# Masked attention scores turned by the DMA crossbar instead of TensorE, with longer leads and loads in smaller steps

## The chip, the cores and the metric

One core of one Trainium2 chip. The metric is the device time of one execution in microseconds (us), the median of several runs.

The profile names the engines PE (TensorE), DVE (VectorE), ACT (ScalarE), POOL (GpSimd) and SP (SyncE). SP only issues DMAs here, one after the other in the order of the program. The DMA share is the time that packets took, as a share of 16 DMA engines; the granted clock is the share of its full clock that TensorE was given.

## The reference, cut to what matters

```python
batch, n_heads, seq, head_dim = 8, 8, 576, 64          # attention
n_tokens, d_model, d_ff = 4608, 512, 2048              # dense layers

scores = scale * np.matmul(q, k.transpose(0, 1, 3, 2))
thresh = np.max(scores, axis=-1, keepdims=True) - tau   # tau = 0.02
scores = np.where(scores >= thresh, scores, -1e9)
attn = np.exp(scores - max)                             # then divided by its sum
x = np.matmul(attn, v)                                  # heads side by side: 4608 x 512
h = x @ w_in
out = (h - np.tanh(h)) @ w_out
```

## The kernel before

It works through 32 pairs of heads. A pair has nine tiles of 128 query rows by 576 keys: four "duos" (an A and a B tile) and one middle tile M made of the remaining rows of both heads. For each tile TensorE computes scores, VectorE scales them and takes the row maximum, and ScalarE masks with a very steep Prelu (`kink`): a score above the threshold passes, one below becomes hugely negative. The masked scores `z` must then be turned, so that keys lie on partitions, before the product with v. Before the change TensorE turns them through an identity matrix into PSUM, and ScalarE takes the exponential from there:

```python
AHEAD = 3                       # scores run three tiles ahead
ps_z = pool("ps_z", 1, space=PSUM)
ps_h = pool("ps_h", 1, space=PSUM)
# ...
def weights(i):
    kd = kind(i % TPP)
    ps = ps_z.tile([P, 5 * P], BF16, name="psZ", tag="z")
    # ... z, pt, off, n by kind of tile: n is 4 (A, M) or 5 (B) ...
    for c in range(n):
        nc.tensor.matmul(
            out=ps[:, c * P : (c + 1) * P],
            lhsT=z[:, off + c * P : off + (c + 1) * P],
            rhs=ident_bf, is_transpose=True, start=True, stop=True,
        )
    # ... one more, half as high, for M ...
    nc.scalar.activation(
        out=pt[:, off : off + n * P], in_=ps[:, 0 : n * P], func=ACT.Exp
    )
# ... per tile s:
scores(s + AHEAD); kink(s + 1); weights(s)
# ... one step of the dense layers: 4 matmuls, then tanh and shrink at once ...
attend(s - 1)                   # product with v
```

From the fifth pair on (tile 39), one step of the dense layers (four 512-column matmuls) is slipped in after each tile; what is left of them follows as a tail. The weights are loaded in 16 pieces of 512 KB during the first 64 tiles. q, k and v come per pair, 256 KB each and the 64 remaining rows of each head apart; a copy of k with its halves swapped (`kS`) is made by two DMAs inside SBUF.

## Time and profile before

| | before |
|---|---|
| time, median of 3 runs | 647.22 us (646.89 to 647.35) |
| span of the profiled run | 644.8 us |
| busy PE / DVE / ACT | 594.6 / 459.5 / 461.6 us |
| attention alone ends (first dense matmul) | 78.1 us |
| tail of dense layers begins | 561.8 us |

The page's lines and the stage table are in the prediction. This is the group view of the hidden layer's matmuls in the kernel before; after the three durations (shortest, median, longest) stand the first and the last start:

```profile
L358 PE MATMUL psH<-xT,w_in_sb x451: 376/379/390, 78.1 to 615.0; 128*128 128x512 bf16 x151
L358 PE MATMUL psHt<-xT,w_in_sb x79: 379/379/379, 561.8 to 613.3; 128*128 128x512 bf16 x79
```

The first `psH` marks the end of the attention-only stage (78.1 us), and the first `psHt`, a buffer name used in the tail alone, the end of the main loop (561.8 us). So the dense stage lasts 483.7 us and the tail 83 us. This is the DMA queue's line of the page; its last figure is the time that its packets took as a share of the span of 16 engines:

```profile
q1 hardware_dynamic: 56662, 56.05, 30.8%
```

### The profile page before, as it was taken

Reading aid. Unit: us, or ns where it says so; the run is one execution under the profiler, and the core shown is the slowest. Engines: PE = TensorE matmul, PEld = TensorE weight load, DVE = VectorE, ACT = ScalarE, POOL = GpSimd, SP = SyncE. Lnnn points to the kernel's source line nnn. Section 1 sums busy time; section 2 is a strip of 40 time slices with the busy share of each in tenths; the row PEclk is TensorE's granted clock in tenths of the full one; section 3 lists DMA queues with packets and bytes.
Section 4 is the critical chain, followed back from the end, with each engine's and each line's share of the span. In section 5 each row is a group of like instructions: output and inputs, shape, how many; then the busy total and the mean of one; then the engine's idle time right before and its main releaser. Section 6 shows DMA issues by size and latency. Waiting matters only on the chain.

```text
span 644.8 us, 15693 instructions
## 1 busy us (share of the span) xinstructions
PE 594.6 (92%) x6048; PEld 362.0 (56%) x6130; DVE 459.5 (71%) x1274; ACT 461.6 (72%) x761; POOL 215.2 (33%) x309
## 2 busy tenths in 40 slices
PE   2988998989999999999999999999999999999990
PEld 2666655556566566656655656656665666544440
DVE  2888888887877777877778777877877777544410
ACT  1888888887778777787778787777778778533410
POOL 6267557733303730343313630362133400000000
PEclk9999999999999999999999999999999999999996
DMA  5565656432223331353133231353134201000111
GB/s 152 155 177 163 175 168 174 119 81 73 64 65 91 104 93 37 93 148 92 40 87 84 77 90 38 93 149 95 36 93 121 66 17 37 18 33 34 49 36 47
DMA packets 57139, 57.35 MB, mean 89 GB/s; under 512 B 20840, under 2 KB 45416, under 8 KB 57064
## 3 DMA queue, kind: packets, MB, share of 16 engines
q1 hardware_dynamic: 56662, 56.05, 30.8%
q8 instruction: 48, 0.79, 0.5%
q10 hardware_dynamic: 402, 0.29, 0.1%
q14 instruction: 27, 0.22, 0.1%
HBM read 37.75 MB, written 9.44 MB: 73 GB/s over the span
## 4 chain that ended last, share of the span: by engine, by line
PE 79%; ACT 9%; DVE 4%; issue 3%; DMA 2%; SPq 1%; ACTq 0%
PE psY L372 18%; PE psH L358 16%; PE psS L228 16%; PE psZ L269 10%; PE psO L313 5%; ACT pT L279 5%; ACT z L253 3%; PE ps_k L172 3%; PE psHt L358 3%; PE ps_q L172 2%; PE psS L218 2%; DVE sc L234 2%; PE psX L337 2%; DMA out_dram<-yo 2%; PE psO L301 1%
## 5 line engine op out<-in xcount | busy, mean ns | idle before, releaser
L279 ACT ACTIVATE pT<-psZ 128x512 f16<-128x512 bf16 (+1 forms) x288 | 184.6, 641 | 83.8 <-PE psZ L269 80.9
L253 ACT ACTIVATE z<-sc,nb 128x576 bf16<-128x576 f32 x288 | 221.3, 768 | 8.9 <-DVE nb L239 8.9
L234 DVE TENSOR_SCALAR_CACHE_REDUCE sc<-psS 128x576 f32<-128x576 f32 x288 | 216.2, 751 | 8.8 <-PE psS L228 7.8
L365 DVE SCALAR_TENSOR_TENSOR g<-th,psH 128x512 bf16<-128x512 f32 x124 | 85.3, 688 | 88.9 <-ACT th L364 88.9
L372 PE MATMUL psY<-w_out_sb,g 128*128 128x512 bf16 x540 | 138.2, 379 | 1.3
L269 PE MATMUL psZ<-ident_bf,z 128*128 128x128 bf16 x1280 | 118.8, 219 | 9.9 <-ACT pT L279 9.1
L358 PE MATMUL psH<-xT,w_in_sb 128*128 128x512 bf16 x451 | 118.1, 379 | 3.4 <-issue 1.3
L269 PEld LDWEIGHTS <-z 128*128 128x128 bf16 x1280 | 79.2, 98 | 52.2 <-issue 16.7
L228 PE MATMUL psS<-kT,qT 128*128 128x512 f16 (+1 forms) x512 | 105.8, 288 | 2.8 <-DVE qT L178 0.9
L228 PEld LDWEIGHTS <-qT 128*128 128x128 f16 x1024 | 74.2, 98 | 58.8 <-issue 5.2
L228 PE MATMUL psS<-kS,qT 128*128 128x512 f16 (+1 forms) x512 | 105.6, 288 | 0.0
L364 ACT ACTIVATE th<-psH 128x512 f32<-128x512 f32 x124 | 74.0, 597 | 35.9 <-PE psH L358 34.3
L146 POOL TENSOR_SCALAR xs<-kraw 128x576 f32<-128x576 f32 x31 | 20.8, 670 | 225.0 <-DMA kraw<-in_k_dram 159.1
L372 PEld LDWEIGHTS <-g 128*128 128x128 bf16 x576 | 51.8, 98 | 46.1
L358 PEld LDWEIGHTS <-w_in_sb 128*128 128x128 bf16 x576 | 51.0, 98 | 43.0 <-issue 0.8
L313 PEld LDWEIGHTS <-pT 128*128 128x128 f16 x1280 | 55.8, 98 | 22.4
L313 PE MATMUL psO<-vb,pT 128*128 128x65 bf16 x1280 | 61.2, 193 | 0.9
L239 DVE TENSOR_SCALAR nb<-mx 128x1 f32<-128x1 f32 x288 | 44.3, 154 | 10.0
L150 POOL TENSOR_TENSOR khl<-xs,khl 128x576 f16<-128x576 f32 x31 | 39.7, 1279 | 2.6
L150 POOL TENSOR_TENSOR qhl<-xs,qhl 128x576 f16<-128x576 f32 x31 | 39.6, 1279 | 2.6
L328 DVE TENSOR_TENSOR osb<-psO,rc 128x320 bf16<-128x320 f32 x64 | 29.3, 458 | 2.2
L178 DVE COPY qT<-ps_q 128x1152 f16<-128x1152 f16 x32 | 24.1, 754 | 9.2 <-PE ps_q L172 9.2
(53 smaller groups left out, 462.3 us busy)
## 6 DMA issues: line engine op xcount, KB each, us to landing
out_dram<-yo SPq DMA_DIRECT2D x36, 256.0 KB
kS<-kT SPq DMA_DIRECT2D x62, 144.0 KB
kraw<-in_k_dram SPq DMA_DIRECT2D x32, 256.0 KB
vraw<-in_v_dram SPq DMA_DIRECT2D x32, 256.0 KB
qraw<-in_q_dram SPq DMA_DIRECT2D x31, 256.0 KB
wt<-in_moe_w_in_dram SPq DMA_DIRECT2D x8, 512.0 KB
wt<-in_moe_w_out_dram SPq DMA_DIRECT2D x8, 512.0 KB
vraw<-in_v_dram SPq DMA_DIRECT2D x64, 32.0 KB
```

The source lines that it names most:

```text
L150: nc.gpsimd.tensor_tensor(out=hl[:, :, 1, :], in0=x, in1=hl[:, :, 0, :], op=ALU.subtract)
L228: nc.tensor.matmul(out=ps[:, dst], lhsT=lhs, rhs=kk[:, src], start=(n == 0), stop=(n == 1),)
L234: nc.vector.tensor_scalar(out=sc, in0=ps[:, lo : lo + S], scalar1=SC, scalar2=None, op0=ALU.mult, op1=ALU.max, accum_out=mx,)
L239: nc.vector.tensor_scalar(out=nb, in0=mx, scalar1=-1.0, scalar2=tau, op0=ALU.mult, op1=ALU.add)
L253: nc.scalar.activation(out=z, in_=sc, func=ACT.Prelu, bias=nb, scale=1.0, alpha=STEEP)
L269: nc.tensor.matmul(out=ps[:, c * P : (c + 1) * P], lhsT=z[:, off + c * P : off + (c + 1) * P], rhs=ident_bf, is_transpose=True, start=True ...
L279: nc.scalar.activation(out=pt[:, off : off + n * P], in_=ps[:, 0 : n * P], func=ACT.Exp)
L313: nc.tensor.matmul(out=po[:, (j - 1 - 5 * hh) + ab, :], lhsT=pt[:, blk * P : (blk + 1) * P], rhs=vb[:, hh, c, :], start=(n == 0), stop=(n ...
L358: nc.tensor.matmul(out=ps, lhsT=w_in_sb[:, c, n * P : (n + 1) * P], rhs=xT[:, c, m, 0:MB] if m < B else xT[:, c, :, MB:S], start=(c == 0), ...
L364: nc.scalar.activation(out=th, in_=ps, func=ACT.Tanh)
L365: nc.vector.scalar_tensor_tensor(out=gs[m][:, n, :], in0=th, scalar=-1.0, in1=ps, op0=ALU.mult, op1=ALU.add,)
L372: nc.tensor.matmul(out=ps, lhsT=gs[m][:, n, ms * P : (ms + 1) * P], rhs=w_out_sb[:, n, :], start=(n == 0), stop=(n == DF_C - 1),)
```

## The change

The intent is to free TensorE, the bound, from the 1312 turns: the DMA crossbar turns a duo of tiles at once, 128x1152, in SBUF, and one exponential reads the turned duo. A turn by DMA comes later than one by TensorE, so the masks now run five tiles ahead of the exponentials and the scores seven. Loads are spread, one tensor a tile; tanh and shrink are put off by a tile; the freed PSUM bank goes to the hidden layer. All loads (but the first q) and all stores stay on the SP queue, with the turns.

```diff
-    AHEAD = 3
+    AHEAD = 7
+    LDK = 16
+    MASK = 5
+    LAG = 2
-    ps_z = pool("ps_z", 1, space=PSUM)
-    ps_h = pool("ps_h", 1, space=PSUM)
+    ps_h = pool("ps_h", 2, space=PSUM)
@@ kink @@
         nc.scalar.activation(
             out=z, in_=sc, func=ACT.Prelu, bias=nb, scale=1.0, alpha=STEEP
         )
+        if kd != "A":
+            n = 5 if kd == "M" else TPP
+            t = zt_pool.tile([P, TPP, P], BF16, name="zT")
+            nc.sync.dma_start_transpose(
+                out=t[:, 0:n, :],
+                in_=zt,
+            )
+            zts[i] = t
@@ weights @@
-        for c in range(n):
-            nc.tensor.matmul(... is_transpose=True ...)      # cut
-        nc.scalar.activation(
-            out=pt[:, off : off + n * P], in_=ps[:, 0 : n * P], func=ACT.Exp
-        )
+        if kd != "A":
+            n = 5 if kd == "M" else TPP
+            pt = p_pool.tile([P, TPP * P], FP16, name="pT")
+            nc.scalar.activation(
+                out=pt[:, 0 : n * P], in_=zts.pop(i)[:, 0:n, :], func=ACT.Exp
+            )
+            pts[i] = pt
@@ main loop, per tile s @@
-        if 0 <= s + 1 < NTILE:
-            kink(s + 1)
+        if 0 <= s + MASK < NTILE:
+            kink(s + MASK)
+        bend()                       # tanh of the step before
         ...
+        shrink()                     # h - tanh(h) of the step before
-        if 0 <= s - 1 < NTILE:
-            attend(s - 1)
+        if 0 <= s - LAG < NTILE:
+            attend(s - LAG)
-            if j == 0 and p + 2 < NPAIR:
-                load(p + 2)          # k, q and v at once
+        for step in plan.pop(s, []): # one tensor's load, split or turn
+            step()
... (cut: nb of the threshold one tile later, x of the dense layers in two tiles,
     stores held back a step, more buffers, other PSUM buffers in the tail)
```

More of the change, by code (lines that the diff above doesn't have):

```diff
@@ L64 @@
     make_identity(nc, ident_bf)
-    xT = const.tile([P, DM_C, B, S], BF16, name="xT")
+    xR = const.tile([P, DM_C, B, S - 512], BF16, name="xR")
     w_in_sb = const.tile([P, DM_C, d_ff], BF16, name="w_in_sb")
     w_out_sb = const.tile([P, DF_C, d_model], BF16, name="w_out_sb")
-    NV = 3
+    NV = 4
     vbs = []
@@ L80 @@
         vbs.append(vb)
+    NM = 2
+    zms = []
+    for i in range(NM):
+        zm = const.tile([P, 5 * P], BF16, name=f"zm{i}")
+        nc.vector.memset(zm[:, S : 5 * P], -STEEP)
+        zms.append(zm)
     pool = lambda name, bufs, **kw: ctx.enter_context(
@@ L88 @@
     qk_pool = pool("qk", 2)
-    sc_pool = pool("sc", AHEAD + 1)
-    st_pool = pool("st", 8)
-    z_pool = pool("z", 3)
+    sc_pool = pool("sc", AHEAD - MASK + 2)
+    st_pool = pool("st", 12)
+    z_pool = pool("z", 4)
+    zt_pool = pool("zt", 4)
     p_pool = pool("p", 3)
@@ L97 @@
     y_pool = pool("y", 2)
+    x_pool = pool("x", 2)
     ps_big = pool("ps_big", 2, space=PSUM)
-    ps_z = pool("ps_z", 1, space=PSUM)
     ps_o = pool("ps_o", 1, space=PSUM)
-    ps_h = pool("ps_h", 1, space=PSUM)
+    ps_h = pool("ps_h", 2, space=PSUM)
     ps_y = pool("ps_y", 1, space=PSUM)
@@ L107, with load @@
     raws = {}
-    def load(p):
+    def load(p, t):
         b, h0 = p // HPAIR, 2 * (p % HPAIR)
         hs = slice(h0, h0 + 2)
-        for t, src in (("k", k), ("q", q)):
-            eng = nc.scalar if p == 0 and t == "q" else nc.sync
-            r = raw_pool.tile([P, 10, D], F32, name=f"{t}raw", tag=t)
-            eng.dma_start(
-                out=r.rearrange("p (h c) d -> p h (c d)", h=2)[:, :, 0 : 4 * D],
-                in_=src[b, hs, 0:512, :].rearrange("h (p c) d -> p h (c d)", c=4),
-            )
-            eng.dma_start(out=r[:, 4, :], in_=src[b, hs, 512:S, :])
-            raws[p, t] = r
-        r = raw_pool.tile([P, 10, D], F32, name="vraw", tag="v")
-        nc.sync.dma_start(
-            out=r[:, 0:8, :].rearrange("p (h c) d -> p h (c d)", h=2),
-            in_=v[b, hs, 0:512, :].rearrange("h (p c) d -> p h (c d)", c=4),
-        )
-        rem = v[b, hs, 512:S, :].rearrange("h s d -> s h d")
-        nc.sync.dma_start(out=r[0:64, 8:10, :], in_=rem)
-        nc.sync.dma_start(out=r[64:P, 8:10, :], in_=rem)
-        raws[p, "v"] = r
+        src = {"k": k, "q": q, "v": v}[t]
+        eng = nc.scalar if p == 0 and t == "q" else nc.sync
+        r = raws[p, t] = raw_pool.tile([P, 10, D], F32, name=f"{t}raw", tag=t)
+        n = 8 if t == "v" else 10
+        eng.dma_start(
+            out=r[:, 0:n, :].rearrange("p (h c) d -> p h (c d)", h=2)[:, :, 0 : 4 * D],
+            in_=src[b, hs, 0:512, :].rearrange("h (p c) d -> p h (c d)", c=4),
+        )
+        if t == "v":
+            rem = src[b, hs, 512:S, :].rearrange("h s d -> s h d")
+            eng.dma_start(out=r[0:64, 8:10, :], in_=rem)
+            eng.dma_start(out=r[64:P, 8:10, :], in_=rem)
+        else:
+            eng.dma_start(out=r[:, 4, :], in_=src[b, hs, 512:S, :])
     hls = {}
@@ L200 @@
     REM = (slice(512, 576), slice(576, 640))
-    scs, zs, pts, ops = {}, {}, {}, {}
+    scs, zs, zts, pts, ops = {}, {}, {}, {}, {}
     def kind(j):
@@ L237, in scores, with shift @@
         )
+        scs[i] = sc, mx
+    def shift(i):
+        sc, mx = scs[i]
         nb = st_pool.tile([P, 1], F32, name="nb", tag="nb")
@@ L247, in kink @@
         if kd == "B":
-            z = zs[i - 1][:, S:W]
-        else:
-            zt = z_pool.tile([P, W], BF16, name="z")
-            zs[i] = zt
+            zt = zs.pop(i - 1)
+            z = zt[:, S:W]
+        elif kd == "A":
+            zt = zs[i] = z_pool.tile([P, W], BF16, name="z")
+            z = zt[:, 0:S]
+        else:
+            zt = zms[i // TPP % NM]
             z = zt[:, 0:S]
@@ L255, in kink @@
         )
+        if kd != "A":
[6 more added lines that the diff above has]
+            zts[i] = t
     def weights(i):
         kd = kind(i % TPP)
-        ps = ps_z.tile([P, 5 * P], BF16, name="psZ", tag="z")
-        if kd == "B":
-            z, pt, off, n = zs.pop(i - 1), pts[i - 1], 512, 5
-        else:
-            z = zs[i] if kd == "A" else zs.pop(i)
+        if kd != "A":
+            n = 5 if kd == "M" else TPP
             pt = p_pool.tile([P, TPP * P], FP16, name="pT")
+            nc.scalar.activation(
+                out=pt[:, 0 : n * P], in_=zts.pop(i)[:, 0:n, :], func=ACT.Exp
+            )
             pts[i] = pt
-            off, n = 0, 4
-        for c in range(n):
-            nc.tensor.matmul(
-                out=ps[:, c * P : (c + 1) * P],
-                lhsT=z[:, off + c * P : off + (c + 1) * P],
-                rhs=ident_bf, is_transpose=True, start=True, stop=True,
-            )
-        if kd == "M":
-            nc.tensor.matmul(
-                out=ps[0:64, 512:640], lhsT=z[:, 512:576],
-                rhs=ident_bf, is_transpose=True, start=True, stop=True,
-            )
-        nc.scalar.activation(
-            out=pt[:, off : off + n * P], in_=ps[:, 0 : n * P], func=ACT.Exp
-        )
-        if kd == "M":
-            nc.scalar.activation(
-                out=pt[0:64, 512:640], in_=ps[0:64, 512:640], func=ACT.Exp
-            )
     def attend(i):
@@ L306, in attend @@
             return
-        pt, hh = pts.pop(i - 1), int(j > 4)
+        pt, hh = pts.pop(i), int(j > 4)
         for ab in range(2):
@@ L331, in norm @@
         )
+    xs = {}
     def emit_x(p):
         o = osb.pop(p)
-        ps = ps_z.tile([P, S], BF16, name="psX", tag="z")
+        ps = ps_h.tile([P, S], BF16, name="psX", tag="h")
         for t in range(4):
@@ L348, in emit_x @@
         b = p // HPAIR
-        nc.vector.tensor_copy(out=xT[:, p % HPAIR, b, :], in_=ps)
-    gs = {}
+        if p % HPAIR == 0:
+            xs[b] = x_pool.tile([P, DM_C, MB], BF16, name="xT")
+        nc.vector.tensor_copy(out=xs[b][:, p % HPAIR, :], in_=ps[:, 0:512])
+        nc.vector.tensor_copy(out=xR[:, p % HPAIR, b, :], in_=ps[:, 512:S])
+    gs, stores = {}, []
     def hidden(m, n, ps):
@@ L359, in hidden, with bend, shrink @@
                 out=ps, lhsT=w_in_sb[:, c, n * P : (n + 1) * P],
-                rhs=xT[:, c, m, 0:MB] if m < B else xT[:, c, :, MB:S],
+                rhs=xs[m][:, c, :] if m < B else xR[:, c, :, :],
                 start=(c == 0), stop=(c == DM_C - 1),
             )
-        th = t_pool.tile([P, MB], F32, name="th")
-        nc.scalar.activation(out=th, in_=ps, func=ACT.Tanh)
-        nc.vector.scalar_tensor_tensor(
-            out=gs[m][:, n, :], in0=th, scalar=-1.0, in1=ps,
-            op0=ALU.mult, op1=ALU.add,
-        )
+        halves.append((m, n, ps))
+    halves, ths = [], []
+    def bend():
+        while halves:
+            m, n, ps = halves.pop(0)
+            th = t_pool.tile([P, MB], F32, name="th")
+            nc.scalar.activation(out=th, in_=ps, func=ACT.Tanh)
+            ths.append((m, n, ps, th))
+    def shrink():
+        while ths:
+            m, n, ps, th = ths.pop(0)
+            nc.vector.scalar_tensor_tensor(
+                out=gs[m][:, n, :], in0=th, scalar=-1.0, in1=ps,
+                op0=ALU.mult, op1=ALU.add,
+            )
     def project(m, ms, part, ps, last):
@@ L383, in project @@
                 rows = out[m * S : m * S + MB, :].rearrange("(p c) n -> c p n", c=4)
-                nc.sync.dma_start(out=rows[ms], in_=yo)
+                to = rows[ms]
             else:
                 rows = out.rearrange("(b s) n -> b s n", b=B)
-                nc.sync.dma_start(out=rows[2 * ms : 2 * ms + 2, MB:S, :], in_=yo)
+                to = rows[2 * ms : 2 * ms + 2, MB:S, :]
+            stores.append(lambda: nc.sync.dma_start(out=to, in_=yo))
     def layers(m, tail):
@@ L393, in h_step @@
         def h_step(n):
-            if tail and n % 3:
+            if tail and n % 2:
                 ps = ps_big.tile([P, MB], F32, name="psHt", tag="big")
@@ L401, in y_step @@
             if part == 0:
-                tag = ("y", "o", "z")[(4 * (m - 1) + ms) % 3] if tail else "y"
-                pl = {"y": ps_y, "o": ps_o, "z": ps_z}[tag]
+                tag = ("y", "o")[ms % 2] if tail else "y"
+                pl = {"y": ps_y, "o": ps_o}[tag]
                 cur["y"] = pl.tile([P, d_model], F32, name="psY", tag=tag)
@@ L440, in w_load @@
         loaded.append((flat, wt, i, cols))
-    load(0)
-    load(1)
+    PREP = (
+        (LDK, lambda p: load(p, "k")),
+        (LDK - 1, lambda p: load(p, "q")),
+        (LDK - 2, lambda p: load(p, "v")),
+        (8, lambda p: split(p, "k")),
+        (7, lambda p: split(p, "q")),
+        (5, lambda p: turn(p, "k")),
+        (3, lambda p: turn(p, "q")),
+        (4, split_v),
+    )
+    plan = {}
+    for p in range(1, NPAIR):
+        first = TPP * p - AHEAD
+        for d, f in PREP[3 if p == 1 else 0 :]:
+            plan.setdefault(first - d, []).append(lambda p=p, f=f: f(p))
+    for t in ("k", "q", "v"):
+        load(0, t)
     for t in ("k", "q"):
@@ L448 @@
     split_v(0)
+    for t in ("k", "q", "v"):
+        load(1, t)
     pieces = w_pieces()
@@ L452 @@
     todo, stage = [], 0
-    for s in range(-AHEAD, NTILE + 4):
+    for at in sorted(plan):
+        if at < -AHEAD:
+            plan.setdefault(-AHEAD, []).extend(plan.pop(at))
+    for s in range(-AHEAD, NTILE + LAG + 3):
         p, j = divmod(max(s, 0), TPP)
-        if 0 <= s < NTILE and j == 3 and p % HPAIR == 0 and p >= HPAIR:
+        if 0 <= s < NTILE and j == 2 + LAG and p % HPAIR == 0 and p >= HPAIR:
             assert not todo
             todo = layers(stage, False)
-            share = len(todo) / (HPAIR * TPP - 3)
+            share = len(todo) / (HPAIR * TPP - 2 - LAG)
             done, stage = 0.0, stage + 1
-        if s + AHEAD < NTILE:
+        if 0 <= s + AHEAD - 1 < NTILE:
+            shift(s + AHEAD - 1)
+        if 0 <= s + AHEAD < NTILE:
             scores(s + AHEAD)
-        if 0 <= s + 1 < NTILE:
-            kink(s + 1)
+        if 0 <= s + MASK < NTILE:
+            kink(s + MASK)
+        bend()
         if 0 <= s < NTILE:
@@ L473 @@
                     done -= 1
-        if s - 1 == NTILE + 1:
-            emit_x(NPAIR - 1)
-        if 0 <= s - 1 < NTILE:
-            attend(s - 1)
-            pp, jj = divmod(s - 1, TPP)
+        shrink()
+        for store in stores[:-1]:
+            store()
+        del stores[:-1]
+        if 0 <= s - LAG < NTILE:
+            attend(s - LAG)
+            pp, jj = divmod(s - LAG, TPP)
             if jj == 4:
@@ L482 @@
                 norm(pp, 1)
-            if jj == 1 and pp > 0:
-                emit_x(pp - 1)
-        if 0 <= s < NTILE:
-            if j == 0 and p + 2 < NPAIR:
-                load(p + 2)
-            if p + 1 < NPAIR:
-                if j == 0:
-                    split(p + 1, "k")
-                if j == 1:
-                    split(p + 1, "q")
-                if j == 2:
-                    split_v(p + 1)
-                    turn(p + 1, "k")
-                if j == 4:
-                    turn(p + 1, "q")
-            if s in w_when:
+        pp, jj = divmod(s - LAG, TPP)
+        if jj == 1 and 0 < pp <= NPAIR:
+            emit_x(pp - 1)
+        for step in plan.pop(s, []):
+            step()
+        if True:
+            if s + AHEAD in w_when:
                 if loaded:
@@ L507 @@
             step()
+            bend()
+            shrink()
+            for store in stores:
+                store()
+            stores.clear()
         stage += 1
```

## The prediction

> **What bounds the kernel now.** I read four views in this order: the page's busy times and slices, the table by stage, the costliest groups, and the chain that ended last in one steady stretch. The page first:
>
> ```profile
> PE 594.6 (92%) x6048; PEld 362.0 (56%) x6130; DVE 459.5 (71%) x1274; ACT 461.6 (72%) x761; POOL 215.2 (33%) x309
> PE   2988998989999999999999999999999999999990
> DVE  2888888887877777877778777877877777544410
> ACT  1888888887778777787778787777778778533410
> DMA  5565656432223331353133231353134201000111
> ```
>
> TensorE is busy 92% of the span; VectorE and ScalarE are next at 71 and 72%; the DMA engines are half busy for the first 120 us and a quarter to a third busy later. The page marks a busy PE as modelled, so I checked it by stage and against the chain.
>
> ```profile
> 20.00:60.00 40.00, 35.27 (x482) 24.78 (x480) 34.03 (x107) 36.24 (x61) 24.84 (x33) 1.00 0.62 179
> 200.00:300.00 100.00, 97.16 (x1041) 60.52 (x1054) 78.81 (x223) 78.94 (x130) 38.09 (x56) 1.00 0.32 86
> 500.00:560.00 60.00, 58.16 (x599) 35.29 (x607) 44.39 (x124) 46.33 (x77) 7.35 (x12) 1.00 0.11 32
> 560.00:600.00 40.00, 39.24 (x181) 17.87 (x185) 17.39 (x26) 14.43 (x25) 0.00 (x0) 1.00 0.11 39
> ```
>
> The columns are window and length, then busy time of PE, weight loads, DVE, ACT and POOL, then granted clock, DMA share and GB/s. Three stages show. Up to about 72 us there are four pairs of heads with attention alone, and ACT (36.2 of 40), PE and DVE are nearly level. From 72 to 558 us attention runs beside the two dense layers and PE alone is full (97 of 100, the two others at 79). From 560 us there are only dense layers, which the change hardly touches.
>
> ```profile
> L269 PE MATMUL psZ<-ident_bf,z 128*128 128x128 bf16 x1280 | 118.8, 219 | 9.9 <-ACT pT L279 9.1
> L253 ACT ACTIVATE z<-sc,nb 128x576 bf16<-128x576 f32 x288 | 221.3, 768 | 8.9 <-DVE nb L239 8.9
> L279 ACT ACTIVATE pT<-psZ 128x512 f16<-128x512 bf16 x160 | 94.8, 592 | 26.1 <-PE psZ L269 23.8 <-PE psZ L275 2.3
> L279 ACT ACTIVATE pT<-psZ 128x640 f16<-128x640 bf16 x128 | 89.8, 702 | 57.7 <-PE psZ L269 57.2
> L349 DVE COPY xT<-psX 128x576 bf16<-128x576 bf16 x32 | 14.5, 454 | 8.0 <-PE psX L344 8.0
> L365 DVE SCALAR_TENSOR_TENSOR g<-th,psH 128x512 bf16<-128x512 f32 x124 | 85.3, 688 | 88.9 <-ACT th L364 88.9
> ```
>
> These are the groups that the change touches: 1280 turns of masked scores on PE, the exponentials that read them from PSUM, and the copy and the shrink that are rearranged. The 118.8 us are not what PE would win, since each turn's 219 ns overlaps its neighbours. The chain in time order has the marginal cost:
>
> ```profile
> 303.04 0.49 PE psS L228 x4
> 303.53 0.22 PE psZ L269 x4
> 303.75 0.86 PE psH L358 x4
> ...
> 308.64 0.49 PE psS L228 x4
> 309.13 0.28 PE psZ L269 x5
> 309.41 0.86 PE psY L372 x4
> ```
>
> Four turns cost 0.22 us and five 0.28 us, so 55 ns each, and the chain stays on PE throughout.
>
> **What the Trainium skill says.** "TensorE: Matmul & The Clock Gate", section "Wait — 56ns, not 53.3ns?", gives 55.6 ns start to start for warm 128-column matmuls; the 0.22 us for four agrees. "DMA: Bandwidth & Descriptors", section "Latency and other measured facts", gives 261 GB/s as the effective rate of a DMA transpose, and the section "Anatomy of one DMA" about 2 us of fixed cost per DMA, measured there on the GpSimd path; no transpose is in this trace, so it cannot confirm the first. "VectorE: DVE Perf Modes", section "The three transpose paths", lists 1309 ns for one 128x128 tile through the crossbar; it does not say whether that is a latency or a rate, and this decides between success and disaster below.
>
> **The change part by part.** Leaving PE: 1280 + 32 turns with their weight loads. Nine tiles make a pair of heads, with 4x4 + 4x5 + 5 = 41 turns; 41 x 55 ns = 2.26 us per pair. The chain from 300 to 318 us gives psZ 14.8% of 18 us, or 2.66 us, since it includes short waits around the turns. I take 2.4 us. The stage table's score count (51.5 tiles per 100 us) makes a pair 17.5 us now, so PE would need about 17.5 x 0.97 - 2.4 = 14.6 us.
>
> ScalarE: 128 pairs of exponentials (592 + 702 ns) become 128 of width 1152. Slope (702 - 592) / 128 = 0.86 ns a column, so an estimated 702 + 512 x 0.86 = 1.14 us against 1.29 us; 32 middle tiles lose a 258 ns piece and pay 110 ns more. That is 24 us by durations, but neighbouring ACT instructions overlap, so I count half: 0.4 us per pair. ACT then needs 78.9/100 x 17.5 - 0.4 = 13.4 us a pair. Tanh one step later no longer makes ACT wait for the matmul just issued.
>
> VectorE: the copy of x splits in two, about 0.1 us more a pair; nb moves one tile later, which removes only idle gaps. 78.8/100 x 17.5 = 13.8 us a pair. The shrink's 88.9 us of idle before it goes, but DVE was not the bound.
>
> SP and DMA: 128 transposes of 128x1152 two-byte elements (295 KB) and 32 of 128x640 (164 KB) come in. At 261 GB/s these are estimates of 1.13 and 0.63 us, so 5.1 us a pair of all 16 engines. The old traffic takes 0.31 x 17.5 = 5.4 us a pair. 10.5 of about 15 us fits. Issue of an ordinary DMA holds SP 0.36 to 0.6 us in the trace; nine loads and copies and a store make about 5.7 us a pair, leaving 9 us for five transposes, about 1.8 us each.
>
> Latency: the mask is five tiles ahead of its exponential. At 1.7 us a tile that is 8.5 us, against an estimated 2 + 1.1 us of transfer, up to 2 us of SP and a few of queueing behind loads. It should hide.
>
> With PE at 14.6 and DVE at 13.8 us I allow 0.7 us for two nearly level in-order engines and take 15.3 us a pair. The 28 pairs after the first four win 28 x (17.5 - 15.3) = 62 us. The first four pairs: compute could fall from 12.4 us a pair (29 tiles in 40 us) to about 11, but the DMA share is 0.62 there already; 0.62 x 12.4 + 5.1 = 12.8 us a pair, so nothing is won. The deeper fill costs perhaps 2 us, the dense tail stays. 647 - 62 + 2 = 587 us. I add 5 us for collisions between transposes and loads: 592 us.
>
> **The rivals.** First, SP or the crossbar takes over. If a 128x128 tile really costs 1.3 us at rate, 41 tiles a pair are 54 us and the kernel would need over 1700 us; that the change puts just five tiles of lead before the exponential speaks against it. If a transpose holds SP 2.5 us rather than under 1.8, SP needs 5 x 2.5 + 5.7 = 18 us a pair and the result is 650 to 670 us. Second, loads delay transposes: the SP queue is in order and also waits for kT and for buffers, and transfers share the engines. Then the exponential waits, ACT and PE follow, and each pair loses 1 to 2 us: 615 to 650 us. For it speaks the 0.62 share early on; against it, that loads now come one tensor a tile. Third, VectorE becomes the bound with no slack at 13.8 us; that is the good end, 28 x 3.2 = 90 us less at most, and about 565 us with some loss.
>
> **Range and chances.** Main case 575 to 605 us, about six in ten. Two in ten go to the second rival, somewhat over one in ten to an SP- or crossbar-bound result above 650 us. So the prediction is 592 us, the range 563 to 652 us, with faster 0.73, same 0.10, slower 0.17.
>
> **What would show it.** Right: psZ gone from PE, PE busy near 520 us in all, no large wait of pT for the transpose, tiles at 1.7 us in the dense stage, the chain still mainly on PE with more DVE. Wrong: pT waiting for zT in many tiles (latency or rate), SP rows back to back with transposes of 2 us or more (SP), a first stage longer than 60 us (DMA crowded), or DVE at 95% with PE idle between its groups. A tail other than 85 us would mean that the new PSUM split matters.

## The result, and the profile after

607.75 us (606.47 to 608.25, 4 runs) against 647.26 us: ratio 0.9388, with a 95% interval of 0.9371 to 0.9404. Ratios here and below are the mean time of one kernel's fast runs over that of the kernel before's fast runs of the same rounds, so not quite the ratio of the medians quoted. Executions over 1.5% slower than the fastest of the same kernel are left out of the means. The output is correct.

Lines of the page of the changed kernel (busy times, then slices, granted clock in tenths, DMA share in tenths):

```profile
PE 526.2 (87%) x4749; PEld 291.4 (48%) x4818; DVE 442.8 (73%) x1311; ACT 439.7 (73%) x601; POOL 215.8 (36%) x310
...
PE   2757576887899999999999999999999999999990
...
DVE  2657465877988898889878888888888888544410
ACT  1576476877998988998798888989898989433310
...
PEclk9888687997999999999999999999999999999996
DMA  4699999999898978999997898899888975111011
```

PE's busy time is down by 68 us. But the slices 2 to 7 (15 to 106 us), which were 8 and 9 before, are 4 to 7 now for PE, DVE and ACT, while DMA is at 9 nearly everywhere. The granted clock falls there too. The stage table, columns as in the prediction; first the one window of the kernel before that the prediction did not show, then the changed kernel:

```profile
60.00:100.00 40.00, 36.19 (x440) 24.18 (x444) 32.70 (x95) 34.09 (x58) 21.17 (x27) 1.00 0.59 174
```

```profile
20.00:60.00 40.00, 25.72 (x260) 14.89 (x258) 26.41 (x84) 25.78 (x33) 17.70 (x23) 0.83 1.02 209
60.00:100.00 40.00, 23.23 (x229) 14.46 (x230) 21.74 (x72) 24.35 (x31) 17.97 (x24) 0.77 1.07 214
200.00:300.00 100.00, 96.97 (x948) 54.99 (x962) 87.22 (x267) 87.31 (x119) 43.51 (x61) 1.00 0.91 188
...
520.00:560.00 40.00, 38.49 (x194) 17.85 (x195) 18.63 (x30) 14.62 (x25) 0.00 (x0) 1.00 0.11 40
```

From 20 to 100 us no compute engine is over 66% busy, and the DMA share passes 1: packets in flight together count twice, so a share near or above 1 is a full queue. In the dense stage PE is at 97% as before, and DVE and ACT have risen from 79 to 87%: more tiles a microsecond. DMA is 91% busy there. The tail is as it was. The marks of the stages in the changed kernel:

```profile
L366 PE MATMUL psH<-xT,w_in_sb x450: 376/379/634, 104.9 to 547.3; 128*128 128x512 bf16 x150
L366 PE MATMUL psHt<-xT,w_in_sb x32: 379/379/379, 524.2 to 549.1; 128*128 128x512 bf16 x32
```

| stage | before | after | difference |
|---|---|---|---|
| attention alone, to the first dense matmul | 78.1 | 104.9 | +26.8 |
| attention and dense layers | 483.7 | 419.3 | -64.4 |
| tail | 83.0 | 82.3 | -0.7 |
| span, us | 644.8 | 606.5 | -38.3 |

So the change wins 64 us where it was meant to and loses 27 us before. What waits in the first stage says why (waits of the changed kernel from 20 to 100 us; us in total, times, longest):

```profile
POOL w_in_sb L448 <- DMA wt<-in_moe_w_in_dram: 40.7, 6, 11.6
ACT pT L285 <- DMA zT<-z: 19.5, 8, 4.7
...
PE psS L236 <- DMA kS<-kT: 17.1, 4, 6.1
```

Weights (24.3 us of waiting before, 40.7 now), turned scores and the swapped copy of k all come late. In the 20 to 100 us of the kernel before, waits of PE and ACT for a DMA are absent from the list. The DMA queue's line after:

```profile
q1 hardware_dynamic: 229718, 99.06, 78.6%
```

0.786 x 606.5 - 0.308 x 644.8 = 278 us more of all 16 engines, for 42.9 MB more (100.21 against 57.35 MB), where the prediction counted 5.1 us a pair, 163 us. (The 278 us are somewhat too many, since the share counts overlapping packets twice.) The exponential of a turned duo, the sole new compute, is as estimated (1.153 us against 1.14), and a turn holds SP for 1.35 us in the median but up to 3.2 us:

```profile
L285 ACT ACTIVATE pT<-zT 128x1152 f16<-128x1152 bf16 x128 | 147.6, 1153 | 40.6 <-DMA zT<-z 40.4
```

```profile
L274 SPq DMA_TRANSPOSE zT<-z x128: 1247/1354/3207, 18.9 to 514.1; - x128
```

### The profile page after: what moved, and what is told of

Its sections match the earlier page's. It is cut to its first block, busy times and chain, and to the rows that moved or that the text cites. A ratio compares the mean times of both kernels' runs of the same rounds, so it can differ in the third digit from the quotient of the medians.

```text
span 606.5 us, 13212 instructions
## 1 busy us (share of the span) xinstructions
PE 526.2 (87%) x4749; PEld 291.4 (48%) x4818; DVE 442.8 (73%) x1311; ACT 439.7 (73%) x601; POOL 215.8 (36%) x310
## 2 busy tenths in 40 slices
DMA packets 230187, 100.21 MB, mean 165 GB/s; under 512 B 193897, under 2 KB 218473, under 8 KB 230121
## 4 chain that ended last, share of the span: by engine, by line
PE 67%; DMA 9%; issue 8%; DVE 7%; POOL 4%; ACT 3%; SPq 0%; POOLq 0%; ACTq 0%; DVEq 0%
PE psY L392 18%; PE psH L366 16%; PE psS L236 15%; PE psO L316 5%; PE ps_k L180 3%; DVE sc L242 3%; PE psS L226 2%; PE psHt L366 2%; DMA wt<-in_moe_w_in_dram 2%; PE ps_q L180 2%; DMA kS<-kT 2%; DMA out_dram<-yo 2%; DMA zT<-z 1%; DMA kraw<-in_k_dram 1%; PE psO L304 1%
## 5 line engine op out<-in xcount | busy, mean ns | idle before, releaser
L268 ACT ACTIVATE z<-sc,nb 128x576 bf16<-128x576 f32 x256 | 193.4, 765 | 30.3 <-DVE nb L251 28.9
L285 ACT ACTIVATE pT<-zT 128x1152 f16<-128x1152 bf16 (+1 forms) x160 | 170.7, 1067 | 44.7 <-DMA zT<-z 40.4
L236 PE MATMUL psS<-kS,qT 128*128 128x512 f16 (+1 forms) x512 | 111.2, 301 | 20.7 <-DMA kS<-kT 20.7
L236 PEld LDWEIGHTS <-qT 128*128 128x128 f16 x1024 | 77.7, 101 | 102.6 <-issue 25.8
L236 PE MATMUL psS<-kT,qT 128*128 128x512 f16 (+1 forms) x512 | 110.3, 299 | 12.7 <-DVE nb L251 6.8
L385 DVE SCALAR_TENSOR_TENSOR g<-th,psH 128x512 bf16<-128x512 f32 x128 | 87.5, 684 | 33.5 <-ACT th L379 33.5
L392 PEld LDWEIGHTS <-g 128*128 128x128 bf16 x576 | 49.6, 98 | 57.7 <-issue 2.5
L366 PEld LDWEIGHTS <-w_in_sb 128*128 128x128 bf16 x576 | 48.9, 98 | 58.2 <-issue 5.7
L268 ACT ACTIVATE zm<-sc,nb 128x576 bf16<-128x576 f32 x32 | 24.7, 773 | 19.2 <-DVE nb L251 19.1
L180 PE MATMUL ps_k<-ident_f,khl 128*128 128x128 f16 x288 | 23.5, 231 | 12.7 <-DVE khl L148 9.1
```

The source lines that it names most:

```text
L180: nc.tensor.matmul(out=ps[:, c * P : (c + 1) * P], lhsT=hl[:, c, :, :].rearrange("p a d -> p (a d)"), rhs=ident_f16, is_transpose=True, st ...
L236: nc.tensor.matmul(out=ps[:, dst], lhsT=lhs, rhs=kk[:, src], start=(n == 0), stop=(n == 1),)
L268: nc.scalar.activation(out=z, in_=sc, func=ACT.Prelu, bias=nb, scale=1.0, alpha=STEEP)
L285: nc.scalar.activation(out=pt[:, 0 : n * P], in_=zts.pop(i)[:, 0:n, :], func=ACT.Exp)
L366: nc.tensor.matmul(out=ps, lhsT=w_in_sb[:, c, n * P : (n + 1) * P], rhs=xs[m][:, c, :] if m < B else xR[:, c, :, :], start=(c == 0), stop= ...
L385: nc.vector.scalar_tensor_tensor(out=gs[m][:, n, :], in0=th, scalar=-1.0, in1=ps, op0=ALU.mult, op1=ALU.add,)
```

## The experiments

Theory A: the gain that is missing was lost in the first stage, because turns and loads fill the DMA engines there. Rivals: B, the deeper leads make the start slow by themselves, since more tiles must be under way before the first is finished; C, the lower TensorE clock from 20 to 100 us is a cause. A rival that no run was made for, the time that SP itself needs to issue so many DMAs, is taken up under w_eighth. Later questions: what the new order alone is worth, why the engines are full, and whether rate or latency holds the dense stage. "First dense matmul" below is read as in the tables above. The diffs are shortened. One edit is left out of them: the runs in which some or all tiles are not turned by the crossbar have five buffers for masked scores instead of four (in pe_first4_lead7 six). In the changed kernel no mask is listed as waiting for such a buffer, so this is no likely cause.

### no_turn: the crossbar's work taken away

```diff
-            t = zt_pool.tile([P, TPP, P], BF16, name="zT")
-            nc.sync.dma_start_transpose(out=t[:, 0:n, :], in_=zt)
-            zts[i] = t
+            zts[i] = zt          # exponential of unturned scores
```

> The changed kernel without its crossbar turns: the exponential reads the masked scores unturned, so the result is wrong on purpose. Theory A (the gain that is missing was lost to crowded DMA engines in the first, attention-only stage): the first matmul of the dense layers comes at 66 to 75 us instead of 104, the DMA share of 20 to 60 us falls from 1.02 to below 0.65, and the time is 568 to 582 us. Theory B (the deeper lead of scores and masks makes the fill slow by itself): the dense layers still start after 95 us and the time stays above 595 us. Theory C (the lower granted clock of TensorE at 20 to 100 us is the cause, not a result): clock below 0.9 in 20 to 100 us here too.

569.29 us, ratio 0.8792 (0.8779 to 0.8805), wrong result. First dense matmul at 77.4 us, dense stage 408.7 us.

```profile
20.00:60.00 40.00, 31.78 (x380) 19.38 (x380) 36.84 (x124) 37.54 (x49) 24.30 (x33) 1.00 0.68 190
```

DVE and ACT are 92 and 94% busy in this window, DMA 0.68. Of the 38 us by which it beats the changed kernel, 27.5 are in the first stage and 10.6 in the dense stage. Theory B falls: with the same leads the first stage takes the old time. The clock is 1.00 here, so the low clock came with the turns and is not needed to explain the loss; whether it added something of its own, this run does not show (PE was only 64% busy at the clock of 0.83). Two expectations were missed: the DMA share is 0.68 and not below 0.65, and I had the dense layers start at 66 to 75 us, but DVE and ACT are nearly full, so even free turns win nothing over the 78.1 us of before.

### order_only: the new order, turned on TensorE

```diff
+    ON_PE = 288                 # all tiles: turned by matmuls into one bank, as before
-    ps_h = pool("ps_h", 2, space=PSUM)
+    ps_h = pool("ps_h", 1, space=PSUM)
+    ps_z = pool("ps_z", 1, space=PSUM)
```

> The new order, leads and pieces of loads, with all scores turned on TensorE as before (one PSUM bank back from the hidden layer to the turns; right result). If the gain comes from taking the turns off TensorE: 638 to 650 us, a pair of heads in the dense stage still near 17.3 us. If a good part comes from the new order (tanh one step later, more lead): 620 to 635 us.

667.07 us, ratio 1.0299 (1.0284 to 1.0314), correct. Slower than before, which neither expectation had: dense stage 498.8 us against 483.7.

```profile
200.00:300.00 100.00, 94.32 (x1009) 58.05 (x1022) 72.38 (x219) 74.73 (x127) 36.15 (x50) 1.00 0.28 76
```

PE falls to 94% in a window where it had 97%. So the new order is no gain by itself; it costs about 20 us when TensorE turns, and going on from there to the crossbar (with the bank that this frees) wins 59 us. What in the order costs 20 us was asked next.

### order_now: tanh and shrink put back

```diff
                     todo.pop(0)()
+                    bend()
+                    shrink()
```

> The new order with all scores turned on TensorE, as in order_only, but tanh and shrink issued right behind their matmuls as in the kernel before (right result). If putting them off by a tile with a single bank for the hidden layer is what made order_only 20 us slower than the kernel before: 643 to 652 us. If the longer leads cost it: 660 to 670 us, as order_only.

668.49 us, ratio 1.033 (1.0314 to 1.0345), correct. The postponement is not the cause. The longer leads are the suspect named in the expectation, but the pieces of loads, the later product with v and the split copy of x changed as well and were not separated, so the cause of these 20 us stays open.

### w_eighth: the weight loads cut to an eighth

```diff
-            nc.sync.dma_start(out=wt, in_=s)
+            nc.gpsimd.memset(wt, 0.01)
+            nc.sync.dma_start(out=wt[:, 0 : cols // 8], in_=s[:, 0 : cols // 8])
```

> The changed kernel with an eighth of the bytes of each weight load (wrong result on purpose; the rest of the tile is set on POOL). Theory A with the weights as the main crowder: the dense layers start at 84 to 92 us instead of 104 and the time is 588 to 596 us. If the crossbar alone fills the engines in the first stage, they start after 98 us and the time is above 602 us.

595.76 us, ratio 0.9194 (0.9181 to 0.9208), wrong result. First dense matmul at 91.9 us, the upper edge of what was expected; dense stage 420.0 us, unchanged.

```profile
20.00:60.00 40.00, 27.66 (x282) 16.81 (x280) 28.52 (x93) 27.23 (x36) 22.04 (x28) 0.87 0.87 178
```

So the bytes of the weights account for 13 of the 27 us lost. The other 14 remain with almost no weights to load and a DMA share of 0.87. Turns and the loads of q, k and v are still too much for a stage that wants a tile every 1.4 us, but what gives out here is not shown. SP is as good a candidate as the DMA engines: its rows in `--timeline --engine SP` sum to 64 of 70 us from 20 us on, and in the changed kernel to 75 of 80, against 33 of 50 before and 32 of 55 in no_turn. By these rows, at the durations without queueing, five turns (four of 1.3 us and one of 1.24), nine loads and copies (5.4 us in no_turn) and the weights (1.1 us) need an estimated 13 us of SP a pair, more than the 12.4 us that a pair took before. No run takes issues off SP in this stage while the crossbar turns there.

### pe_first4: TensorE turns where it has time

```diff
+    ON_PE = 36
     def weights(i):
+        if i < ON_PE:
+            return turn_on_pe(i)     # matmuls into a ps_h bank, as the kernel before
-        if kd != "A":
+        if kd != "A" and i >= ON_PE:
             ...                      # the crossbar's turn
```

> The changed kernel, but the 36 tiles of the first four pairs, whose stage has no dense layers, are turned on TensorE through one of the two banks of the hidden layer; the crossbar from tile 36 on (right result). Theory A: the dense layers start at 74 to 82 us, the time is 580 to 588 us, better than both kernels. Theory B: still after 95 us, 600 us or more.

584.58 us, ratio 0.9037 (0.9011 to 0.9063), correct, and better than both kernels. First dense matmul at 78.5 us, dense stage 421.8 us.

```profile
20.00:60.00 40.00, 37.08 (x502) 25.83 (x500) 35.78 (x116) 36.88 (x63) 24.00 (x32) 1.00 0.65 187
60.00:100.00 40.00, 31.45 (x357) 19.61 (x357) 30.85 (x101) 32.69 (x49) 23.16 (x30) 0.96 0.94 216
```

The first line is the old kernel's first stage again (clock 1.00, PE, DVE and ACT about 90%); the second has the crossbar's first turns. This is theory A's own prediction, and it came true: moving back 164 of the 1312 turns wins another 23 us. It shows that the turns cost the first stage its time, but it relieves SP and the DMA engines alike.

### xbar_alone: the disputed transfers by themselves

The kernel body is replaced by 32 transfers of each kind, back to back on SP, with a fence after each kind:

```diff
+    stages = (turn(9),), (turn(5),), (turn(1),), (copy,), (main,), (rem,), (rem16,),
+             (turn(9), main), (turn(9), rem), (turn(9), rem16), (turn(9), copy)
+    for st in stages:
+        for i in range(32):
+            for f in st: f(i)
+        fence()                  # VectorE reads the last one
```

> The disputed transfers by themselves, 32 of each kind back to back on the SP queue with nothing else running (wrong result on purpose): turns of 128x1152, 128x640 and 128x128, a plain copy of 128x1152 in SBUF, the 256 KB load of q, its 32 KB of remaining rows as now and split in two, then the large turn alternating with each. The excess of DMA time in the changed kernel (78.6% of 606 us against 30.8% of 645 us, 278 us over 128 x 72 + 32 x 40 = 10496 blocks of 16x128) says 26 ns a block. If the crossbar itself is that slow: about 1.9 us for each large turn alone, 1.05 us for the middle one. If it runs at the 261 GB/s of the prediction: 1.1 and 0.6 us alone, and only the mixed stages are slow: then a turn with a load costs over 1 us more than the two alone. If the remaining rows, whose source has two in its outer dimension, run on two of the engines only, a turn alternating with them costs over 1 us more than with them split.

Wrong result. From fence to fence, divided by 32:

| 32 times | us each |
|---|---|
| turn 128x1152 (295 KB) | 1.50 |
| turn 128x640 | 1.37 |
| turn 128x128 | 1.32 |
| copy 128x1152 in SBUF | 0.84 |
| load of q, 256 KB | 0.78 |
| remaining rows of q, 32 KB, one DMA | 0.88 |
| the same in two DMAs | 1.24 |
| large turn + load | 2.11 |
| large turn + remaining rows | 2.34 |
| large turn + remaining rows in two | 2.75 |
| large turn + copy | 2.35 |

Windows inside the stages (large, middle and small turn, copy; remaining rows; turn with remaining rows, with them in two; last columns clock, DMA share, GB/s):

```profile
6.00:46.00 40.00, 0.00 (x0) 0.00 (x0) 1.00 1.09 206
54.00:90.00 36.00, 0.00 (x0) 0.00 (x0) 1.00 0.61 123
98.00:134.00 36.00, 0.00 (x0) 0.00 (x0) 1.00 0.13 26
141.00:160.00 19.00, 0.00 (x0) 0.00 (x0) 1.00 1.02 387
...
188.00:215.00 27.00, 0.32 (x2) 0.00 (x0) 1.00 0.16 37
...
330.00:398.00 68.00, 0.00 (x0) 0.00 (x0) 1.00 0.93 145
405.00:484.00 79.00, 0.00 (x0) 0.00 (x0) 1.00 0.64 123
```

Neither of the two rates expected holds, and the remaining rows beside a turn cost less in one DMA than in two, not over 1 us more. A turn costs SP about 1.3 us at each of the three sizes, as the small ones show with a share of 0.13. The large one just fills the engines (share 1.09) at 206 GB/s, 1.44 us for 295 KB, where the prediction had 1.13 us and a plain copy runs at 387 GB/s. Mixed transfers cost about the sum of the parts (2.11 us against 2.28 for the turn with the load, the others within 0.05 us). That is remarkable for the remaining rows. The Trainium skill, "DMA: Bandwidth & Descriptors", section "Why a DMA increments its semaphore by 16 and not by 1", has a DMA run on as many engines, up to 16, as divide the outer dimension of both sides; here 128 and 2 (two heads), so two. The share of 0.16 alone agrees (2 of 16 are 0.125, and overlapping packets count twice). And yet a turn with them takes the full 0.84 us longer, with the share at 0.93. Not all of this is the engines: by SP's rows the issue alone needs about 1.3 + 0.53 us and two gaps of 0.05, 1.9 of the 2.34 us. The other 0.4 us show in the turn's own rows, 1.71 us in the median here against 1.39 for turns alone: SP is held up in them. That fits a turn that needs all engines and finds two of them busy with the remaining rows; the trace does not show the engines one by one, so this is a reading. Split in two, the share is 0.64: there SP's issue is the limit (1.3 + 1.2 us).

### rem16 and pe_first4_rem16: the remaining rows on all engines

```diff
-            eng.dma_start(out=r[:, 4, :], in_=src[b, hs, 512:S, :])
+            for hh in range(2):
+                eng.dma_start(
+                    out=r[64 * hh : 64 * hh + 64, 4, :], in_=src[b, h0 + hh, 512:S, :]
+                )
```

> The changed kernel with the 64 remaining rows of k and of q loaded as two pieces of one head each, so that no load runs on two DMA engines alone (right result; two more DMAs a pair for SP). If turns are held up behind those two engines: DMA share in 200 to 500 us falls below 0.8 and the time to 590 to 602 us. If the crossbar's own rate fills the engines: 606 to 612 us, unchanged or a little worse.

616.39 us, ratio 0.9527 (0.949 to 0.9565), correct: 8.6 us slower than the changed kernel.

> Both: first four pairs turned on TensorE, and the remaining rows split. If those rows held up turns: 572 to 580 us, near the 569 us of the kernel without turns. If not: 583 to 588 us, as with the first change alone.

597.11 us, ratio 0.9223 (0.9204 to 0.9242), correct: 12.5 us slower than pe_first4. In both the gain did not come, and both times lie outside either expectation; the dense stage got longer (432.5 us and 436.0 us). SP's own rows in the changed kernel sum to 110 us of 120 from 200 to 320 us, so two more DMAs of 0.6 us a pair are not free. Whether SP is then the limit was tried next.

### pool_loads and pool_loads_rem16: the loads on the POOL queue

```diff
-        eng = nc.scalar if p == 0 and t == "q" else nc.sync
+        eng = nc.scalar if p == 0 and t == "q" else nc.sync if p < 2 else nc.gpsimd
```

> First four pairs turned on TensorE as in pe_first4, and from the third pair on the loads of q, k and v issued from the POOL queue instead of SP, the same bytes through the same engines (right result). If the SP queue, busy issuing about 110 of 120 us in the dense stage, is what keeps that stage some 13 us longer than without turns: 570 to 579 us. If the DMA engines are: 582 to 588 us, as pe_first4. If issuing costs POOL too much: above 590 us.

611.37 us (608.0 to 615.06), ratio 0.9451 (0.94 to 0.9502), correct: 27 us slower than pe_first4, although SP has seven DMAs a pair less. Dense stage 445.2 us.

```profile
L275 SPq DMA_TRANSPOSE zT<-z x112: 1242/1701/5467, 68.7 to 515.7; - x112
```

A turn now holds SP for 1.70 us in the median and up to 5.5 us, and exponentials wait 28.5 us for turned scores from 200 to 500 us, against 10.3 us in pe_first4: SP stands in the turn instead of in its own loads. That loads of a second queue in the same engines cause this was not tested. The third case of the expectation, that issuing costs POOL too much, fits as well: from 200 to 300 us POOL is 75% busy, against 40% in pe_first4, with 0.64 to 0.85 us for each load that it issues. The two were not separated.

> As pool_loads, with the remaining rows of q and k split over all engines. In the SP-bound reading of rem16, the split hurt only because it put 1.2 us more a pair on SP, and freed two engines otherwise: now 568 to 578 us and not slower than pool_loads. If the split hurts by itself: 8 to 12 us slower than pool_loads.

588.94 us (585.57 to 594.16, the three fast runs; a slow one took 599.38), ratio 0.9109 (0.9048 to 0.917), correct. With the loads off SP the split is worth 22 us, where on SP it cost 12.5. The first half of the expectation holds in direction, though the time is above its 568 to 578 us: it fits that the remaining rows hold up turns, and that splitting them hurts only by SP's time. But the kernel is still slower than pe_first4, and its fast runs scatter by 9 us. So neither taking loads off SP nor splitting those rows gave a better kernel; of those tried, the ones with all on one queue and the rows unsplit are the best.

### lead3 and pe_first4_lead7: less and more lead

```diff
-    AHEAD = 7          # lead3, from the changed kernel
-    MASK = 5
+    AHEAD = 5
+    MASK = 3
-    AHEAD = 7          # pe_first4_lead7, from pe_first4 (and a buffer more of z and zT)
-    MASK = 5
+    AHEAD = 9
+    MASK = 7
```

> The changed kernel with three tiles of lead between mask and exponential instead of five, scores five ahead instead of seven (right result). If the turn's latency under load is about the predicted 5 us, three tiles of 1.7 us just cover it: 608 to 625 us. If it is 8 us or more, as waits of up to 4.9 us behind a lead of five tiles suggest, the exponential waits in most tiles: over 640 us, slower than before.

653.59 us, ratio 1.0111 (1.0074 to 1.0147), correct. That is 46 us slower than the changed kernel.

```profile
L366 PE MATMUL psH<-xT,w_in_sb x438: 376/379/634, 104.0 to 592.0; 128*128 128x512 bf16 x146
L366 PE MATMUL psHt<-xT,w_in_sb x32: 379/379/379, 568.9 to 593.7; 128*128 128x512 bf16 x32
```

The first dense matmul is at 104.0 us, as with five tiles of lead (104.9), but the dense stage lasts 464.9 us instead of 419.3. So the first stage is held by a rate (of the DMA engines or of SP's issue), since lead makes no difference there, and the dense stage is a matter of latency: exponentials wait 93 us for turned scores there, against 16 us with five tiles of lead, so three tiles of 1.7 us do not cover a turn.

> pe_first4 with seven tiles of lead between mask and exponential instead of five and scores nine ahead, one more buffer each for masked and turned scores (right result). If what is left of the waits for turns in the dense stage is latency (16.8 us of waiting exponentials there in pe_first4): 570 to 580 us. If the stage is held by rate, of DMA engines 94% busy or of TensorE: 582 to 588 us, unchanged.

579.97 us (579.61 to 583.11), ratio 0.8969 (0.8941 to 0.8998), correct: the best kernel, though only 4.6 us below pe_first4 by medians. It was run at another time. PE is 98 to 99% busy from 200 to 500 us and the dense stage lasts 414.8 us, against 421.8 for pe_first4 and 408.7 with no turns at all.

## Why the prediction was right, and where it was off

It named 592 us and got 607.75, inside its range and faster as it said. By its steps:

- **Turns off TensorE, pair at 15.3 us, 62 us won in 28 pairs.** Right in the total: the dense stage is 64.4 us shorter, or 419.3 / 28 = 15.0 us a pair, and PE's busy time is 526 us where 520 was named. But some of the agreement is luck. In order_only the new order, with its turns still on TensorE, made the dense stage 15.1 us longer; from there the turns and the freed bank win 79.5 us. The prediction had neither this loss nor so large a gain, and the two nearly cancel. 55 ns a turn (63 us in 28 pairs) was nearer than the group's busy time of 118.8 us (104 us in 28 pairs), but it was not confirmed by itself.
- **ScalarE and VectorE below PE.** Right: 1.153 us for the long exponential; DVE and ACT at 87%.
- **"Nothing is won" in the first four pairs.** This is the term that was mis-sized. Its sum was 0.62 x 12.4 + 5.1 = 12.8 us of DMA a pair. From 20 to 100 us the slot is 80 us for 41 tiles, 17.6 us a pair, and the stage lost 26.8 us. Two of the inputs are measured now. Five turns a pair cost 4 x 1.44 us and, at a share of 0.61, 0.84 us: 6.6 us and not 5.1. And two DMAs of remaining rows a pair cost 2 x 0.84 us of turning time, which the average share of 16 engines hid. That makes about 15.7 us (0.62 x 12.4 = 7.7, less 0.3 for those rows' own share, plus 1.7 and 6.6). The remaining 1.9 us a pair were not traced to a cause, and part of the 1.7 us is SP's issue (xbar_alone). SP was left out of the prediction's sum for this stage: it was counted for the dense stage alone, and without the weights. Its estimated 13 us a pair already exceed the old 12.4, so how much of the loss is the engines' and how much SP's stays open. The averaged share was an error of method: it doesn't show whether a few engines are busier than the others. Nor could its sign of being wrong, a first stage longer than 60 us, tell anything: the stage took 78.1 us before.
- **Latency "should hide".** Right in the large, not in the estimate of about 5 us with some queueing: with three tiles of lead (about 5 us) the kernel loses 46 us, and seven still win a little over five.
- **SP under 1.8 us a turn.** Right in the median (1.35 us). But with all that it waits in its turns, SP is busy 110 of 120 us, so it has little time for more pieces (rem16).
- **The rivals.** The second, loads and turns that delay each other, took place, but mainly in the first stage: there it cost 27 us, while the dense stage is only 10.6 us longer than without turns. The first did not happen as it was put, for the crossbar: a 128x128 turn does take 1.32 us, but a turn nine times as large takes 1.50 us, so the 1309 ns are not a rate. For SP it is open in the first stage, as said. The third did not come; its sum was off as well, since from 17.5 to 13.8 us a pair would be 28 x 3.7 = 104 us and not 90.

## What to carry to other kernels

Before moving work to an engine that is idle on average, add up its demand stage by stage, with the rate of that very transfer measured alone, and the time that the queue needs to issue it; here one stage won 64 us and another lost 27 by the same edit. Where a stage has the old engine idle, leave the work there: choosing by stage won 23 us more for a few lines. And give a DMA in the middle of a chain a lead in tiles that covers its latency under load, which was over 5 us here.

## What the Trainium skill lacked or had wrong

- "DMA: Bandwidth & Descriptors", section "Latency and other measured facts": 261 GB/s for a DMA transpose with a middle dimension that is not contiguous, about 350 to 400 GB/s for a contiguous one. Here, below both, 206 GB/s for 128x1152 two-byte elements from SBUF to SBUF with nothing beside it, full engines. "Advanced Engine Details and Errata", section "X-Bar Transpose (TRN2)", has transposes as fast as regular DMAs: 206 against 387 GB/s for a plain copy of the same tile here.
- "VectorE: DVE Perf Modes", section "The three transpose paths": 1309 ns for 128x128 by the crossbar agrees with 1.32 us here, but it doesn't say that this is nearly the same for nine times the data (1.50 us).
- No page has that a transpose and a DMA on few engines about add up: 2.34 us together, 1.50 and 0.88 alone, though the latter uses a share of 0.16. SP's issue alone would need about 1.9 us of it.
- "DMA: Bandwidth & Descriptors", section "Issuing engines are not separate DMA queues", says that a second issuing engine only saves sequencer time. Here it also cost: with the loads on the POOL queue a turn held SP for 1.70 us instead of about 1.35 in the median, POOL was 75% busy instead of 40%, and the kernel went from 584.58 to 611.37 us; which of the two cost it is not shown.
